# A gated mix of sliding-window attention and a token MLP: a new written order, a 128-column last piece, gate logits off TensorE

## The chip, the cores and the metric

The kernel runs on one core of a Trainium2 chip. The metric is the device time of one execution in microseconds; the median of three executions of the kernel before is 200.21 us (199.88 to 200.73). A core has five engines that run side by side [...]: TensorE (PE; its weight loads are listed apart as PEld), ScalarE (ACT), VectorE (DVE), GpSimd (POOL), and SyncE (SP), which here issues all DMA transfers. Matrix products land in PSUM, eight banks of 128 partitions by 512 fp32 values; all other on-chip data is in SBUF.

## The reference, cut to what matters

S = 2048 tokens, D = 512, 32 heads of 16, a window of 256 keys, F = 1376 hidden units. All inputs and the output are bf16.

```python
g = sigmoid((x * gate_w).sum(-1, keepdims=True))          # one gate per token
q, k, v = heads(x @ wqkv)                                 # 32 heads of 16
p = softmax(where(0 <= i - j < 256, q @ k.T / 4, -1e9))   # i query token, j key token
a = (p @ v) @ wo
h = layernorm(x)                                          # the same x as above
u = gelu(einsum("bsd,sf->bdf", h, w1) + b1)               # the MLP mixes tokens, not features
b = transpose(einsum("bdf,fs->bds", u, w2) + b2)          # back to tokens by features
return g * a + (1 - g) * b
```

## The kernel before, in words

Tokens are cut into 16 tiles of 128 and into 4 blocks of 512. The work is a list of named tasks. Each task belongs to one engine and issues one or a few instructions:

- `xta0.n.g` and `xtc0.n.g`: TensorE transposes of the first four token tiles (four 128x128 transposes each) and their copies to SBUF, line 606 and 599. The other three blocks are loaded already transposed by DMA (`xt1` to `xt3`).
- `q`, `k`, `v` chains (`project`, line 700; `chain`, line 653): products over four chunks of D. A chain is cut into steps; `q1_0.2` is the step of chain q1 of block 0 that begins with product 2. For block 0 the first weight chunk is applied to tokens 0 to 255 and 256 to 511 in two products of 256 columns, so these chains have five steps. `qc`, `kc`, `vc` are the copies out of PSUM; `qc` multiplies by a parity pattern so that two heads share a product.
- `sj.v0` to `sj.v3`, `sj.C`: scores of query tile j, and of the corners of its window (lines 923 and 1017); `e...` their exponentials on ACT, `m...` the window masks (line 901), on DVE or POOL; `pvj.i` the products with V (line 1073); `n1` to `n4` and `nz` the transposes and scalings on DVE that bring the result back into `xo`.
- `bs`, `ba`, `pow`, `h`: layernorm statistics and result. `u0` to `u10`: the first MLP product, 16 products a chain in steps of two. `ub`: its bias. `gelu`: one pass over all of it on ACT. `y0` to `y14`: second MLP product (11 products) and the attention's `wo` product (4) in one PSUM bank, `f` the final scale and bias, `o` the store. Tile 15 is cut into two pieces of 256 columns, `y15l` and `y15r` (line 1282).
- The gate's logits: for the first `NGP` = 1 blocks by 16 TensorE products with one column each (`gate0`, line 797), for the others by `gl`, one multiply with accumulation on DVE per token tile, which reads `gwr`, a copy of `gate_w` in every partition (load `gw`). `gatem` limits, `gatee` exponentiates, `ez` spreads them.

TensorE works in several tilings. A plain step uses the whole array. Score steps use four strips of 32 rows, `pv` steps four strips of 32 columns, corners both. A step of `q`, `k`, `v`, `u` or `y` is issued plain, or, where the name of the attention step before it stands in `THEN`, as four products of 32 output columns each, which then run side by side. In what follows "tiled steps" are these.

**What sets the order.** Each engine's order is written out by hand in `PLAN` (line 189), with the PSUM bank or buffer number that a task takes after the colon. `arrange` (line 85) only merges the five lists: it walks them with assumed costs (`SWITCH`, `LATENCY`, `BLOCK`) and decides the order in which instructions are emitted between engines, and where a POOL task gets a wait for a recent DVE task (line 1312 on). The order on each engine is that of `PLAN`. Every engine runs its list strictly in order, so a task that waits holds up all behind it.

**Start.** DVE clears `zeros`, 128x512 in the later `ug` buffer; TensorE multiplies zeros (`warm`, five products of 512 columns, `warmb`, three of 256; line 589) while the first loads are under way. SP issues `x0.0 x0.2 wqk0 wqk1 wqk2 wqk3 x1.4 xt1 wv x2.8 bias xt3 ...` in this order.

## Time and profile before

| | |
|---|---|
| median of the runs | 200.21 us |
| the profiled execution's own time | 199.82 us |
| its span (first to last instruction) | 198.1 us |
| PE busy | 193.0 us, 4058 products |
| ACT busy | 169.0 us |
| DVE busy | 156.5 us |
| POOL busy | 80.0 us |
| products with a full-clock record | from 6.92 us on |

How to read it: a product is issued before the one ahead of it has drained, so busy times of PE overlap and a busy PE is not PE at its peak. The distance from the start of one task's first product to the start of the next task's first product is what a task costs the PE queue. The groups list an instruction's busy time, its mean duration, and the idle time of its engine before it. 1.72 us of the profiled execution lie outside the span.

### The profile page before, as it was taken

The numbers are of one execution on the slowest core, as the hardware profiler recorded it, in microseconds if no ns is written. First come the engines' busy times: TensorE is split into PE (matmuls) and PEld (weight loads), VectorE is DVE, ScalarE is ACT, GpSimd is POOL, SyncE is SP. The second block draws the span as 40 slices with busy tenths as digits, with TensorE's granted clock in tenths as the row PEclk, the third lists the DMA queues.
The fourth block names the chain that finished last, engine by engine and source line by source line (L and its number), as shares of the span: only waits on it lengthen the run. The fifth ranks groups of instructions, "written<-read, shape, count | busy, mean of one in ns | idle before, by whom it ended". The sixth has DMA issues, their size and how long they took to land. (4 is left out here: it accounts for less than half of the span.)

```text
span 198.1 us, 9100 instructions
## 1 busy us (share of the span) xinstructions
PE 193.0 (97%) x4058; PEld 93.3 (47%) x4058; DVE 156.5 (79%) x318; ACT 169.0 (85%) x198; POOL 80.0 (40%) x118
## 2 busy tenths in 40 slices
PE   7999999999999999999999999999999999999993
PEld 3643444353635445446543554344445354554572
DVE  1799888879998988986589799636867868869683
ACT  2369999999988996998999899899899989898632
POOL 6394897525344440214223200045069335452310
PEclk9999999999999999999999999999999999999999
DMA  5999798970060000001399770000211220200002
GB/s 156 294 284 232 131 319 278 346 187 0 8 174 18 18 0 3 3 5 32 98 364 367 280 210 3 26 26 30 68 37 58 60 68 22 62 30 30 30 3 83
DMA packets 23189, 22.02 MB, mean 111 GB/s; under 512 B 7566, under 2 KB 21262, under 8 KB 23150
## 3 DMA queue, kind: packets, MB, share of 16 engines
q1 hardware_dynamic: 23150, 21.44, 36.9%
q8 instruction: 32, 0.52, 1.1%
q14 instruction: 7, 0.06, 0.1%
HBM read 15.61 MB, written 2.10 MB: 89 GB/s over the span
## 5 line engine op out<-in xcount | busy, mean ns | idle before, releaser
L894 ACT ACTIVATE et<-ps 128x1024 bf16<-128x1024 f32 (+1 forms) x94 | 89.3, 1015 | 6.1 <-PE ps L942 2.4
L536 POOL TENSOR_SCALAR_AFFINE_SELECT et<-et 128x512 bf16<-128x512 bf16 (+2 forms) x63 | 46.7, 751 | 56.0 <-ACT et L894 40.9
L894 ACT ACTIVATE XT<-ps 128x1024 bf16<-128x1024 f32 (+1 forms) x60 | 58.1, 1011 | 7.3 <-PE ps L942 4.3
L670 PEld LDWEIGHTS <-wb 128*32 128x32 bf16 (+4 forms) x645 | 32.0, 97 | 34.5 <-issue 6.5
L670 PE MATMUL pb<-ug,wb 128*32 128x512 bf16 (+4 forms) x385 | 45.5, 366 | 0.0
L670 PE MATMUL pb<-h,wb 128*128 128x512 bf16 (+2 forms) x260 | 44.5, 381 | 0.0
L536 POOL TENSOR_SCALAR_AFFINE_SELECT XT<-XT 128x512 bf16<-128x512 bf16 (+1 forms) x28 | 20.0, 720 | 46.3 <-ACT XT L894 27.4
L670 PE MATMUL pb<-XT,wqkv 128*128 128x512 bf16 (+2 forms) x190 | 32.4, 372 | 0.4 <-DMA wqkv<-in_A_wqkv_dram 0.3
L1178 DVE STREAM_TRANSPOSE et<-ps 128x1024 f32<-128x1024 f32 (+1 forms) x17 | 20.1, 1183 | 11.9 <-PE ps L1087 11.1
L1087 PEld LDWEIGHTS <-VA 128*32 128x32 bf16 (+1 forms) x1056 | 20.1, 97 | 6.6 <-issue 1.5
L942 PE MATMUL ps<-QZ,KT 32*128 32x256 bf16 (+1 forms) x496 | 23.1, 265 | 0.0
L754 DVE TENSOR_TENSOR QZ<-pb,par 128x1024 bf16<-128x1024 f32 x16 | 19.5, 1221 | 3.2 <-PE pb L670 3.2
L670 PEld LDWEIGHTS <-wqkv 128*128 128x128 bf16 (+1 forms) x190 | 12.7, 98 | 14.6 <-DMA wqkv<-in_A_wqkv_dram 0.5
L670 PE MATMUL pb<-wo,xo 128*32 128x512 bf16 (+2 forms) x152 | 18.1, 375 | 0.0
L1087 PE MATMUL ps<-et,VA 128*32 128x128 bf16 (+2 forms) x624 | 17.9, 218 | 0.0
L942 PEld LDWEIGHTS <-KT 32*128 32x128 bf16 x496 | 7.4, 92 | 20.6 <-ACT et L894 10.7
L670 PE MATMUL pb<-wqkv,XT 128*128 128x512 bf16 (+1 forms) x70 | 16.5, 381 | 0.0
L974 DVE TENSOR_TENSOR et<-et,mask 128x512 bf16<-128x512 bf16 x26 | 13.3, 510 | 2.5 <-ACT et L894 2.4
L441 DVE TENSOR_SCALAR ot<-pb,c,c 128x512 bf16<-128x512 f32 (+1 forms) x11 | 8.6, 785 | 7.4 <-PE pb L670 7.3
L1087 PE MATMUL ps<-XT,VA 128*32 128x128 bf16 (+2 forms) x432 | 13.9, 215 | 0.0
L1087 PEld LDWEIGHTS <-VZ 128*32 128x32 bf16 x832 | 13.2, 98 | 0.7
L770 DVE BATCH_NORM_STATS2 stats<-xo 128x6 f32<-128x512 bf16 x16 | 10.7, 682 | 3.1 <-DMA xo<-in_A_x_dram 3.1
(76 smaller groups left out, 199.4 us busy)
## 6 DMA issues: line engine op xcount, KB each, us to landing
wb<-in_B_w_dram SPq DMA_DIRECT2D x8, 512.0 KB, 8.2
wb<-in_B_w_dram SPq DMA_DIRECT2D x2, 2048.0 KB, 9.2
VZ<-VA SPq DMA_DIRECT2D x26, 70.0 KB, 3.0
xo<-in_A_x_dram SPq DMA_DIRECT2D x3, 512.0 KB, 5.5
out_dram<-ot SPq DMA_DIRECT2D x12, 128.0 KB, 2.4
wb<-in_B_w_dram SPq DMA_DIRECT2D x4, 352.0 KB, 5.8
wqkv<-in_A_wqkv_dram SPq DMA_DIRECT2D x4, 256.0 KB, 5.0
wb<-in_B_w_dram SPq DMA_DIRECT2D x1, 1024.0 KB, 5.3
```

Source lines behind the costliest of these rows:

```text
L441: return nc.vector.tensor_scalar(out=out_, in0=in_, scalar1=scale, scalar2=bias, op0=ALU.mult, op1=ALU.add)
L536: return nc.gpsimd.affine_select(out=out_, in_=in_, pattern=[[0, n] for n in pattern] + [[step, HB]], compare_op=op, fill=0.0, base=base_, ...
L670: made.append(nc.tensor.matmul(buf(b)[c:z_, c0:c0 + w_], lhsT=lhsT[:, c:z_], rhs=rhs, start=(j == 0), stop=(j == n - 1), skip_group_check= ...
L754: lambda k=k, b=b: nc.vector.tensor_tensor(out=QZ[:, k, :, (i % NQ) * SB:(i % NQ + 1) * SB], in0=buf(b)[:, None, :].to_broadcast([P, 2, SB ...
L770: f"bs{t_}", {"DVE": 0.67}, lambda b=b, t_=t_: nc.vector.bn_stats(buf(b)[:], xo[:, t_, :]),
L894: lambda e=e, b=b, shape=shape: nc.scalar.activation(out=shape(buf(e)), in_=shape(buf(b)), func=ACT.Exp, scale=SCALE),
L942: made.append(nc.tensor.matmul(to[:, :, done:done + m], lhsT=keys(j if x == "A" else j - 1, k)[rows], rhs=q[rows], start=True, stop=True, ...
L974: made.append(nc.vector.tensor_tensor(out=v, in0=v, in1=m.to_broadcast(list(v.shape)), op=ALU.mult))
L1087: return lambda: nc.tensor.matmul(to(), lhsT=v() if callable(v) else v, rhs=buf(e)[rows, col:col + n], start=first, stop=last, tile_positi ...
L1178: lambda: nc.vector.transpose(out=view(buf(tr).bitcast(FP32)), in_=view(buf(o))), [last], takes=[tr], uses=[o],
```

## The change

1. `y15r` is cut into `y15m` and `y15r`, 128 columns each, with their own final scaling and store.
2. `zeros` is 128x128; the warming products read it four (or two) times over with a stride of zero. They have the same count and width.
3. `NGP` is 0: `gate0` is gone, and `gl0` to `gl3` join DVE's list. `gw` is issued much earlier.
4. All lists of `PLAN`, and `THEN`, are written anew: the order on every engine, the banks, and which of the copies and masks run on which engine. POOL has 12 `m...v` masks fewer and one corner mask more; DVE 12 more and one fewer.
5. The assumed costs of `arrange` are refined (`TURN`, `cost_of`, the cost of `gelu`).

The halves of the first Q and K products are in both kernels, since `project` is the same. What differs is their place: before, nine halves stand ahead of the first later step (`q1_0.2`), now thirteen, with `xta0.1.1` moved in behind the first four of them.

```diff
-SWITCH = 0.095
-BLOCK, AHEAD, FETCH, BUSY = 256, 80, 3.6, 3.0
-LATENCY = {"PE": 0.22, "ACT": 0.15, "DVE": 0.12, "POOL": 0.15, "SP": 2.0}
+TURN = {
+    "d": dict(d=0, s=0.100, p=0.100, c=0.098, h=0.100),
...
+BLOCK, AHEAD, FETCH, BUSY = 256, 80, 3.1, 3.5
+LATENCY = {"PE": 0.21, "ACT": 0.15, "DVE": 0.11, "POOL": 0.12, "SP": 2.0}
+def cost_of(t, e):
...
-            if new != mode:
-                t.cost += SWITCH
+            t.cost += TURN[mode][new]
...
 PLAN = dict(
     PE="""
-        warm:3 xta0.0.0:7 xta0.0.1:6 warmb xta0.1.1:4 xta0.1.0:5 q1_0.0:2 k3_0.0:3 k1_0.0:6 q3_0.0:1 k0_0.0:7
-        q3_0.1 q0_0.0:0 k3_0.1 q1_0.1 q1_0.2 k1_0.1 k3_0.2 k0_0.1 q0_0.1 q2_0.0:5 q1_0.3 q0_0.2 q1_0.4 q0_0.3
+        warm:5 xta0.0.0:6 xta0.0.1:4 warmb xta0.1.0:3 q3_0.0:2 q2_0.0:5 k1_0.0:6 q1_0.0:1 xta0.1.1:4
+        k0_0.0:7 k3_0.0:0 q3_0.1 k3_0.1 k0_0.1 q2_0.1 k1_0.1 q0_0.0:3 q1_0.1 q3_0.2 k3_0.2 q0_0.1 q3_0.3
...
-        y14.11 y14.13 y13.13 y15r.6 y15r.8 y15l.11 y15l.13 y15r.10 y15r.11 y15r.13
+        y14.11 y15l.4 y15m.2 y15l.6 y15m.4 y15m.6 y14.13 y15l.8 y15l.10 y15l.11 y15l.13 y15m.8 y15m.10
+        y15m.11 y15m.13 y15r.0:3 y15r.2 y15r.4 y15r.6 y15r.8 y15r.10 y15r.11 y15r.13
...
     DVE="""
-        const zeros bs3:1 xtc0.0.0 bs2:0 ba3 parity bs1:1 ba2 ba1 bs0:0 ba0 qc1_0 bs4:1 qc0_0 ba4 qc3_0 qc2_0 qc3_1
+        const zeros parity bs0:0 bs3:1 ba3 xtc0.0.1 xtc0.0.0 xtc0.1.0 bs1:1 ba0 ba1 bs2:0 qc3_0 bs5:1 qc0_0
+        qc1_0 gl0 gl1 ba2 qc2_0 ba5 bs6:0 ba6 gl3 h2 vc5 gl2 gatem0 h3 bs4:0 qc3_1 ba4 bs7:1 bs8:0 biasc ba8
...
     SP="""
-        x0.0 x0.2 wqk0 wqk1 wqk2 wqk3 x1.4 xt1 wv x2.8 bias xt3 x3.12 xt2 vs0 w1_02 w1_03 vs1 w1_22 vs2 gw w1_12
+        x0.0 x0.2 wqk0 wqk3 wqk1 wqk2 x1.4 wv gw xt1 xt3 bias x2.8 vs0 xt2 w1_20 w1_12 vs1 x3.12 w1_03 vs2
...
-    NGP = 1
+    NGP = 0
...
-    zeros = ug[:, 0, :]
+    zeros = ug[:, 0, 0:P]
...
-            nc.tensor.matmul(buf(wu)[:, 0:w], lhsT=zeros[:, 0:P], rhs=zeros[:, 0:w], start=True, stop=True)
+            nc.tensor.matmul(
+                buf(wu)[:, 0:w].rearrange("p (a b) -> p a b", b=P), lhsT=zeros,
+                rhs=zeros[:, None, :].to_broadcast([P, w // P, P]), start=True, stop=True,
+            )
...
-        parts = [("", 0, D)] if t_ < NT - 1 else [("l", 0, D // 2), ("r", D // 2, D)]
+        parts = [("", 0, D)] if t_ < NT - 1 else [("l", 0, D // 2), ("m", D // 2, 3 * D // 4), ("r", 3 * D // 4, D)]
```

## The prediction

> **What bounds the kernel.** I read the page's busy shares first, then the waits of TensorE, then the timeline of TensorE and of the tail.

> The busy shares:
> ```profile
> PE 193.0 (97%) x4058; PEld 93.3 (47%) x4058; DVE 156.5 (79%) x318; ACT 169.0 (85%) x198; POOL 80.0 (40%) x118
> ```
> PE is listed as busy all the time, which alone says little, since products overlap. TensorE's own waits say more:
> ```profile
> PE pb L591 <- DVE ug L518: 1.4, 1, 1.4
> PE pb L670 <- DMA wqkv<-in_A_wqkv_dram: 0.3, 1, 0.3
> PE pb L670 <- ACT XT L894: 0.2, 1, 0.2
> ```
> Three waits in 198 us: for the zeros, for the first weights, and once for ACT. So from the first real product at 6.57 the kernel is a TensorE queue with hardly a hole, and its time is: start of that queue, sum of the steps, tail. The prices of the steps are distances between starts in the timeline of PE (start, length, instruction):
> ```profile
> 23.02 0.54 PE L802 MATMUL pb<-gwc,XT 128*128 128x1 bf16 x16
> 23.43 1.02 PE L670 MATMUL pb<-wqkv,XT 128*128 128x512 bf16 x4
> ...
> 30.68 0.59 PE L670 MATMUL pb<-XT,wqkv 128*128 128x512 bf16 x2
> 31.21 0.41 PE L1087 MATMUL ps<-et,VA 128*32 128x128 bf16 x16
> ...
> 56.84 1.47 PE L670 MATMUL pb<-h,wb 128*128 128x512 bf16 x6
> 58.24 0.40 PE L942 MATMUL ps<-QZ,KT 32*128 32x256 bf16 x8
> 58.57 1.68 PE L670 MATMUL pb<-h,wb 128*128 128x512 bf16 x7
> ```
> The gate's 16 products cost 0.41. A plain step of two products, followed by another, costs 0.432 (median of the steps); followed by strips of columns 0.53 (30.68 to 31.21), so that change of tiling costs 0.10. Six products and a change take 1.40 (3 x 0.432 + 0.10), a score step 0.33. The tail:
> ```profile
> 194.40 0.60 PE L670 MATMUL pb<-wo,xo 128*128 128x256 bf16 x4
> ...
> 195.04 0.55 DVE L441 TENSOR_SCALAR ot<-pb,c,c 128x256 bf16<-128x256 f32 x1 [0.61 <-PE pb L670]
> ...
> 195.61 0.33 SPq L1305 DMA_DIRECT2D out_dram<-ot  x1
> ```
> Last product out at 195.00, final scaling to 195.59, store, end at 198.1.

> I laid the medians of such distances, per kind of step and kind of the next one, under the whole list of before: 186.62 from 6.57 to the end of the last product's slot. The trace takes 188.26. The 1.64 between are waits too small to be listed: 0.16 while the clock comes up (two halves at 0.19 for 0.109), 0.25 at `s10.v0`, 0.13 at `y9.6`, 0.11 at `pv1.3`, 0.08 at `k0_3.2`, 0.07 at `y1.2`, the rest crumbs.

> [...] 256 zero columns take 0.213 at 4.6, 256 real ones 0.109 after 7.0, and the full-clock record starts at 6.92. [...] the trace has no plain 128-column product at full clock. [...] the gate's products, each with a 128x128 weight load, pass at 25 ns, so the load is no floor. [...] The last store has rows of 512 B before, 256 B after; no run here shows the latter.

> **The change, part by part, on the queue of PE.**

> Gate: `gate0` leaves, -0.40. `gl0` to `gl3` come to DVE at 0.7 to 0.8 each (the accumulating multiply is 8.3 us for 12, and its read-out 81 ns), 3.1 in all; 12 masks `m...v` move from POOL to DVE at 0.45 to 0.51 (5.7), one corner mask goes back. DVE gets some 8 us more on 156.5 of 198, POOL loses as much. This costs nothing while DVE keeps ahead of the bank it must free; without that cover it would cost up to the 3.1 at the start, where DVE has 9.58 of 10 us busy between 10 and 20. I followed that stretch: `qc1_0` ends about 13.5, `gl0` and `gl1` 14.8, `qc2_0` 16.0, `gl3` and `h2` 17.8, `vc5` 18.4; PE wants the bank of `vc5` (`v14.0`) at 19.2. Covered by 0.8.

> Changes of tiling: 167 before, 163 after. Every score, corner and `pv` group still has its own; what goes is four direct changes between plain and tiled steps (13 to 9), -0.40. Tiled steps are 67, not 74; leaving a tiled step costs 0.107 rather than 0.095, and that happens 22 times, not 27: -0.06.

> Last tile: 15 products of 256 columns become 30 of 128. By the slope between 512 and 256 columns, 0.416 ns a column, one is 0.056: 30 x 0.056 - 15 x 0.109 = +0.05. [...] I take 0.05, for the 25 ns above.

> Start: the weights `wqk0` land at 6.53 in both, so the first product stays at 6.57. But before, all 16 transposes are over by then; after, `xta0.1.1` stands behind four products: 4 x 0.056 = +0.22 at full clock (0.43 at half). The weights now come as 0, 3, 1, 2, landing at 6.53, 7.19, 7.84, 8.44 by the trace. The first step with chunk 1, `q3_0.2`, comes up at 8.21, the first with chunk 2 at 8.76: 0.3 to spare. The shorter clearing of zeros (0.27 for 512 columns, so some 0.15 less) lets warming start earlier, hidden behind `x0.0`, which lands at 3.74.

> SP queue: `wv` and `gw` now go ahead of `xt1`. By the pace of 512 KB in 1.7 us (8.44 to 10.12) `wv` lands near 12, wanted at 12.75 (`v0.0`); `xt1` about 2.3 later than the 12.05 of before, so 14.3, wanted at 15.9 (`v5.0`). `vs13` waits for `vc13` (about 35.7) and holds `w1_13`, `w1_01`, `w1_00` behind it until 37 to 39; at 1.7 each the last lands about 43, wanted at 46 (`u3.0`). All hidden, the thinnest by 0.7.

> Sum of the steps after, rounding included: 186.00, thus -0.62. Tail: the scaling of 128 columns is 0.13 shorter (0.81 at 512, 0.55 at 256)[...]. The middle piece is scaled on ACT and issued before the last is scaled, so SP is free.

> Small waits: 1.48 of before beyond the clock's 0.16. The new order has its own. Two are in sight: after gelu, ACT frees bank 6 for `s9.v3` some 0.15 to 0.2 late, and `s9.v2` after it 0.1 late (gelu with its two table loads takes 7.8; the exponentials follow at 0.905 each); and `y15l.11` comes 2.67 after `pv15.2`, whose way through DVE takes 2.8. That makes 0.4; I give the rest another 1.1, so as many as before. The profiled execution goes from 199.82 to 199.07. The median of the runs lies 0.39 above it: 199.46, said as **199.4**.

> **Rivals.** Half a per cent, 1.0 us here, is about what a measurement can tell from no change: faster means under 199.2, slower over 201.2.

> *The waits shrink.* If the new order has 0.4 of small waits instead of 1.5, the time is 198.4. For it: between 13 and 31 I find ACT and DVE ready 0.1 to 0.5 ahead of every bank that PE wants. Against: 0.1 is little, and some will fail.

> *The waits grow.* PE comes earlier to gelu and to each score step while ACT's 169 us stay; DVE has 8 more. One microsecond more of waits gives 200.4, no change; it needs 0.1 at ten of the 60 score steps.

> [...]

> [...] Before 6.92, PE idles 0.46 between the last transpose and the first product; after, with `xta0.1.1` gone from there, 0.89. [...] It decides once the full-clock record starts past about 10 rather than near 7. Against it: the warming itself is unchanged[...].

> That the change does not do what it says is true in part: the halves are in both kernels; only their order changed, priced above.

> **How the numbers follow.** Forecast 199.4 (198.9 to 199.9): 0.40, a little over half below 199.2. Waits shrink: 0.20. Waits grow: 0.24, of it 0.04 beyond 201.2. [...] Clock late: 0.10. Faster 0.22 + 0.20 = 0.42; slower 0.10 + 0.04 = 0.14; the rest, 0.44, is no change. The range 198.3 to 201.0 leaves out the late clock, the tail of the growing waits and some 0.04 below.

> **What would show it.** Right: L802 gone from PE; first real product at 6.5 to 6.6; the full-clock record near 7; the last product out about 0.6 earlier than 195.00; the last scaling near 0.42; the 128-column products 0.056 apart. Wrong: waits of PE on ACT or DVE that add up to over 2.5 us, a wait on `wqkv`, `XT` or `wb` loads, a full-clock record near 10, or a last store that takes over 0.3 longer from issue to the end.

## The result

The kernel after takes 205.46 us, median of four executions (204.32 to 205.84), against 200.47 of four of the kernel before (199.88 to 201.06). The ratio is 1.0258, with a 95% interval of 1.0228 to 1.0289. It is slower by 5 us; the forecast was 199.4, with a range up to 201.0. Single executions of a kernel can run over 1.5% above its fastest one; the ratios here and below leave these out, the medians include them.

The profiled execution took 205.32 us with a span of 203.6. From the page of after, the busy times and the chain of work that ended last by engine:
```profile
PE 193.9 (95%) x4018; PEld 92.5 (45%) x4018; DVE 158.3 (78%) x338; ACT 168.3 (83%) x198; POOL 72.6 (36%) x108
...
PE 79%; DMA 12%; SPq 4%; ACT 2%; issue 2%; DVE 0%; ACTq 0%
```
TensorE is no longer busy without a break: 95% of a longer span, and the chain leaves it for transfers (DMA 12%) and for "issue", time in which an engine waited for nothing that the profile shows. The waits of TensorE of after (instruction and line, what ended the wait, us in total, times, longest):
```profile
PE ps L1115 <- issue: 2.1, 3, 1.2
PE pb L698 <- DMA wqkv<-in_A_wqkv_dram: 1.2, 2, 0.9
PE pb L616 <- DVE ug L543: 1.2, 1, 1.2
PE pb L698 <- DMA wb<-in_B_w_dram: 1.0, 2, 0.5
PE ps L1115 <- DMA VZ<-VA: 0.9, 1, 0.9
PE pb L636 <- DMA xo<-in_A_x_dram: 0.3, 1, 0.3
PE ps L970 <- issue: 0.2, 1, 0.2
```
The waits of before held three lines, two of them of the start and one of 0.2. Here five lines are new (both on "issue", and those on `wb`, `VZ` and `xo`), and the one on `wqkv` has grown from 0.3 to 1.2. Apart from the wait for the zeros at the start, no wait on ACT or DVE, which the prediction's rivals spoke of, is among them.

I laid the prediction's step prices under the trace of after, as was done for before. The sum of the differences is the span's difference:

| | before | after | difference |
|---|---|---|---|
| first real product | 6.57 | 6.08 | -0.49 |
| steps, by their prices | 186.62 | 186.00 | -0.62 |
| waits between them | 1.64 | 8.53 | +6.89 |
| end of the last slot to the end of the span | 3.26 | 2.98 | -0.28 |
| span | 198.1 | 203.6 | +5.5 |

The steps are taken at the prediction's prices here, so that line checks nothing by itself; the single prices are compared further down. The tail moved the way that was worked out. What the prediction took as equal grew by 6.9 us. The waits by place, the step named being the first that comes late:

| step | us | what is late |
|---|---|---|
| `q3_0.3` | 1.03 | load of `wqk2`, landed at 9.26 |
| `u3.0`, `u7.0` | 0.68, 0.65 | loads `w1_00`, `w1_10`, landed at 47.3 and 51.5 |
| `pv7.1` to `u9.14` | 1.23 | copy `vz7`, landed at 114.2 and 114.4 |
| `u6.2`, `pv8.2`, `y14.4`, `pv15.2` | 0.43, 1.34, 0.74, 0.69 | nothing that the profile shows |
| all others | 1.74 | as many as before |

So 3.6 us are transfers, 3.2 have no releaser. Both kinds can be seen in the timeline of TensorE of after (start, length, operation, tiles, count, idle time before it and what ended it):
```profile
113.10 0.23 PE L1115 MATMUL ps<-XT,VA 128*32 128x128 bf16 x4
114.20 0.41 PE L1115 MATMUL ps<-et,VZ 128*32 128x64 bf16 x8 [0.87 <-DMA VZ<-VA]
...
118.09 0.20 PE L1115 MATMUL ps<-et,VZ 128*32 128x64 bf16 x2
119.44 0.23 PE L1115 MATMUL ps<-et,VZ 128*32 128x64 bf16 x6 [1.16 <-issue]
```
The second wait falls in the middle of eight products of one kind on the same tiles: two went, six followed 1.35 us later. None of the six has a semaphore to wait for in the trace.

**The transfers.** SP's queue in the timeline of after, around `vs13`:
```profile
25.72 0.59 SPq L511 DMA_DIRECT2D wb<-in_B_w_dram  x1
36.62 0.46 SPq L746 DMA_DIRECT2D VS<-VA  x1
37.13 1.76 SPq L747 DMA_DIRECT2D VS<-VA  x1
38.93 1.70 SPq L511 DMA_DIRECT2D wb<-in_B_w_dram  x3
...
42.01 1.50 SPq L511 DMA_DIRECT2D wb<-in_B_w_dram  x2
```
SP stands from 26.3 to 36.6 for `vc13`, and five loads of `w1` stand behind it. That is as predicted. The prediction followed the first three of them and let the last of these, `w1_00`, land at 43; it landed at 47.3. The fourth, `w1_10`, landed at 51.5. And around `vz7`:
```profile
104.16 0.37 SPq L1301 DMA_DIRECT2D wb<-in_B_w_dram  x1
104.59 0.51 SPq L756 DMA_DIRECT2D VZ<-VA  x1
105.14 0.59 SPq L757 DMA_DIRECT2D VZ<-VA  x1
```
`w2_1`, 2 MB, is issued just ahead of the two copies of `vz7`, so they share the queue with it and take 9.6 and 9.2 us. The pages give the median of all such copies from issue to landing, first before, then after:
```profile
VZ<-VA SPq DMA_DIRECT2D x26, 70.0 KB, 3.0
```
```profile
VZ<-VA SPq DMA_DIRECT2D x26, 70.0 KB, 7.1
```
In before `vz7` was issued behind the other 2 MB load, `w2_0`, and its first copy took 9.1 us too; but that was at 96.46, and it landed at 105.54, well ahead of its use. What the new order changed is how late it stands.

**The waits without a releaser.** Instructions are data too: the page of after lists two DMA queues of the kind "instruction". The larger of them, in after and then in before (packets, MB, share):
```profile
q8 instruction: 31, 0.51, 1.1%
```
```profile
q8 instruction: 32, 0.52, 1.1%
```
Each packet is of 16384 bytes. In after 31 come with 8036 weight loads and products, from the first packet to the last one per 258 of them on the mean; in before, with 32, one per 254. So I take this queue for TensorE's, and a packet for 256 rows of TensorE's list, which is the `BLOCK` of the kernel's own planner. Such packets need not cost anything: in before no wait of TensorE is put down to "issue". The records of the queue in the trace of after say when they do. For each wait without a releaser: TensorE's place in its list of instructions, the last packet before it, and when TensorE went on:

```
row of the list   row mod 256   packet          goes on    after its end
2477              173           76.87-77.80     79.19      1.39
4266              170           117.08-118.06   119.44     1.38
7585              161           189.29-190.83   192.16     1.33
7841              161           193.21-194.31   195.89     1.57
```
All four stand at nearly the same place of a block, and TensorE goes on 1.3 to 1.6 us after the packet's end. For three of the four the packet starts 1.0 to 1.2 us after TensorE has entered the block before it; for the one at `pv8.2`, with the loads of `w2_2` under way, it started 2.4 us after. A packet takes 0.9 to 1.5 us. Added up, 1.05 + 0.95 + 1.4, my estimate is that a block has to last 3.4 us, or TensorE waits for the rest, and longer where the packet starts or moves more slowly. The blocks ahead of these four waits lasted 2.9, 3.45 (`pv8.2`), 3.3 and 3.1 us; the shortest of before, 3.43, ended without one. A plain step of 0.43 us uses 4 of the 256, a tiled one 16, but a group of 128 `pv` products in 1.36 us uses them all. The mean over the kernel is 6 us a block; whether two dense groups fall into one block and the next is a matter of where the boundaries lie. The estimate is my reading of one trace; the experiments below put it to the test.

### The profile page after: what moved, and what is told of

Same layout as the page of the kernel before. It is cut to its first block, busy times and chain, and to the rows that moved or that the text cites. A ratio compares the mean times of both kernels' runs of the same rounds, so it can differ in the third digit from the quotient of the medians.

```text
span 203.6 us, 9014 instructions
## 1 busy us (share of the span) xinstructions
PE 193.9 (95%) x4018; PEld 92.5 (45%) x4018; DVE 158.3 (78%) x338; ACT 168.3 (83%) x198; POOL 72.6 (36%) x108
## 4 chain that ended last, share of the span: by engine, by line
PE 79%; DMA 12%; SPq 4%; ACT 2%; issue 2%; DVE 0%; ACTq 0%
PE pb L698 57%; PE ps L1115 10%; PE ps L970 8%; DMA VZ<-VA 5%; DMA wb<-in_B_w_dram 5%; DMA wqkv<-in_A_wqkv_dram 3%; PE ps L1070 2%; SPq L747 1%; SPq L511 1%; ACT et L922 1%; SPq L495 1%; ACT XT L922 1%; SPq L479 0%; ACT VA L630 0%; PE ps L1026 0%
## 5 line engine op out<-in xcount | busy, mean ns | idle before, releaser
L922 ACT ACTIVATE et<-ps 128x1024 bf16<-128x1024 f32 (+1 forms) x104 | 98.4, 1012 | 8.0 <-PE ps L970 3.7
L561 POOL TENSOR_SCALAR_AFFINE_SELECT et<-et 128x512 bf16<-128x512 bf16 (+2 forms) x57 | 42.4, 755 | 73.0 <-ACT et L922 47.5
L922 ACT ACTIVATE XT<-ps 128x1024 bf16<-128x1024 f32 (+1 forms) x50 | 49.5, 1032 | 5.3 <-PE ps L970 5.3
L698 PE MATMUL pb<-h,wb 128*32 128x512 bf16 (+2 forms) x326 | 45.0, 381 | 1.0 <-DMA wb<-in_B_w_dram 1.0
L698 PE MATMUL pb<-ug,wb 128*32 128x512 bf16 (+6 forms) x309 | 45.2, 362 | 0.0
L561 POOL TENSOR_SCALAR_AFFINE_SELECT XT<-XT 128x512 bf16<-128x512 bf16 (+3 forms) x24 | 17.3, 731 | 41.2 <-DVE et L935 12.5
L698 PE MATMUL pb<-wo,xo 128*32 128x512 bf16 (+3 forms) x168 | 17.9, 370 | 0.0
L698 PE MATMUL pb<-wqkv,XT 128*128 128x512 bf16 x64 | 16.7, 381 | 0.0
L935 DVE TENSOR_TENSOR et<-et,mask 128x1024 bf16<-128x1024 bf16 (+1 forms) x19 | 12.0, 646 | 4.9 <-ACT et L922 4.9
L1115 PE MATMUL ps<-et,VZ 128*32 128x64 bf16 x608 | 13.0, 193 | 2.0 <-issue 1.2
```

The lines of the kernel that those rows point to most:

```text
L561: return nc.gpsimd.affine_select(out=out_, in_=in_, pattern=[[0, n] for n in pattern] + [[step, HB]], compare_op=op, fill=0.0, base=base_, ...
L698: made.append(nc.tensor.matmul(buf(b)[c:z_, c0:c0 + w_], lhsT=lhsT[:, c:z_], rhs=rhs, start=(j == 0), stop=(j == n - 1), skip_group_check= ...
L922: lambda e=e, b=b, shape=shape: nc.scalar.activation(out=shape(buf(e)), in_=shape(buf(b)), func=ACT.Exp, scale=SCALE),
L935: return nc.vector.tensor_tensor(out=v, in0=v, in1=m[:, None, :].to_broadcast([P, n, w]), op=ALU.mult)
L1115: return lambda: nc.tensor.matmul(to(), lhsT=v() if callable(v) else v, rhs=buf(e)[rows, col:col + n], start=first, stop=last, tile_positi ...
```

## The experiments

Ratios are against runs of the kernel before on the same chip.

### The transfers, one at a time

```diff
 vz7_first:
-        vz8:1 w2_1 vz7:0 vz11:2 w2_2
+        vz8:1 vz7:0 w2_1 vz11:2 w2_2
```

> The kernel after, with one change in SP's list: the two copies of vz7 are issued ahead of the 2 MB load w2_1 instead of behind it. Theory of the queue: pv7.1 waited 0.9 us for VZ because its copies sat behind w2_1 (issued 104.6, landed 114.4, where such copies took 3 us in the kernel before). The wait on VZ goes, u9.14 starts about 1.2 us earlier, and with it gelu and the y steps: about 1.2 us faster than the kernel after (205.5 to 204.3). Rival, a hidden wait: gelu, the last w2 load or ACT sets the start of y4.0 anyway, the wait moves to y4.0 or s9.v1 and under 0.4 us is won.

203.93 us, 1.0135 (1.0045 to 1.0224), with executions from 201.68 to 205.50. The wait on `VZ` is gone. `pv8.2`, on the same stretch, waits 0.48 in place of 1.34.

```diff
 vs13_late:
-        w1_02 vs13 w1_13 w1_01 w1_00 vz2:1 w1_10 w1_11 vz6:2
+        w1_02 w1_13 w1_01 w1_00 vz2:1 w1_10 w1_11 vs13 vz6:2
```

> The kernel after, with one change in SP's list: the copies vs13, which wait for vc13 until 36.6 us, are issued behind w1_11 instead of ahead of w1_13, w1_01, w1_00, w1_10, w1_11. Theory of the queue: SP stood from 26.3 to 36.6 and these five loads came 10 us late; u3.0 waited 0.68 us and u7.0 0.65 us for them. Both waits go: about 1.3 us faster than the kernel after (to 204.2). Rival: PE at 46 to 51 us is also held by ACT (score banks), so that the waits on wb go but 0.5 us or more comes back as waits on ACT at s3 and s4.

204.99 us, 1.0208 (1.0145 to 1.0270). The waits at `u3.0` and `u7.0`, 1.33 us, are gone from the profile, yet the median fell by 0.5 only, which four executions from 202.73 (the profiled one) to 205.43 can't tell from nothing. `pv8.2` now waits 1.53, and `pv7.1` 1.1. In the profiles each order of SP does what it was made for, and `vs13_late` gives a part of what it earns back behind it.

### Two attempts at the waits without a releaser

```diff
 untile: THEN without these
-    s5.v0 s8.v2 pv7.0 pv7.1 pv14.1 pv14.3
 uncluster: the four steps of pv8 moved from between pv7.2 and q3_3.0
-        pv7.2 pv8.0:6 pv8.1 pv7.3 pv8.2 pv8.3 q3_3.0:5
+        pv7.2 pv7.3 q3_3.0:5
-        q1_3.2 k0_3.2 y4.0:3
+        q1_3.2 k0_3.2 pv8.0:6 pv8.1 pv8.2 pv8.3 y4.0:3
```

> The kernel after, with six names taken out of THEN (s5.v0, s8.v2, pv7.0, pv7.1, pv14.1, pv14.3): the q, u and y steps after them are issued plain, two instructions pairs instead of eight. Nothing is left out of the computation. Theory of instruction supply: PE takes its instructions in blocks of 256 from DRAM (31 packets of 16 KB on the instruction queue), a block arrives some 2.4 us after it is asked for, and dense stretches of pv and tiled steps use a block up in 1.4 us; the stretches at u6.2 (0.43 us), pv8.2 (1.34), y14.4 (0.74) and pv15.2 (0.69) waited for that. With fewer instructions in front, u6.2, y14.4 and pv15.2 lose most of their waits and pv8.2 part of it: 1.2 to 2.0 us less waiting, some 0.8 us given back by about eight more changes of tiling; net 0.4 to 1.2 us faster than the kernel after. Rival, a semaphore that the profile does not show (banks, masks on POOL or DVE): the waits stay within 0.2 us of where they are, and the kernel is 0.8 us slower than after.

> The kernel after, with the four steps of pv8 moved from between pv7.2 and pv7.3 to behind k0_3.2, seven q and k steps later; all else is as it was. Theory of instruction supply: pv7.2 to pv8.3 are 320 pairs of instructions within some 1.8 us of work, more than a block; with 3 us of q and k steps between them the 1.34 us wait inside pv8.2 goes and the kernel is 1.0 to 1.4 us faster than after. Rival (pv8 waits for its own inputs, VZ copies vz8 or masks m8): those were long there by the trace, but if it is so, the wait inside pv8 stays where pv8 goes or shrinks by the 3 us that it is later, with PE idle for another releaser; a second rival, n18 on DVE three us later holds bank 6 for s9.v1 and gives back 0.5 us or more.

`untile`: 211.74 us, 1.0561 (1.0514 to 1.0607). `uncluster`: 209.44 us, 1.0459 (1.0427 to 1.0491). Both missed by far. In `untile` the waits at `u6.2`, `y14.4` and `pv15.2` went; the one at `pv8.2` moved on into `pv8.3` and doubled, and others came at places that nothing had been done to. From its timeline of TensorE, one that is new and the one in `pv8.3`:
```profile
98.59 0.29 PE L1115 MATMUL ps<-et,VA 128*32 128x128 bf16 x6 [1.39 <-issue]
...
124.44 0.35 PE L1115 MATMUL ps<-et,VA 128*32 128x128 bf16 x12 [2.67 <-issue]
```
In `uncluster`, `pv8` still waits 0.6 inside, and a new wait of 1.4 without a releaser comes at 189.7. But a part of its loss is not of that kind. From its waits,
```profile
PE pb L698 <- DVE et L1206: 1.5, 1, 1.5
```
is the wait of `y4.0` on DVE, which had itself stood 4.83 us for the result of `pv8`. That is close to the second rival that was named, though it hits another step. And behind this wait TensorE's granted clock was 0.5 from 123.91 to 127.32: products of 512 columns came 0.43 apart in place of 0.216, some 1.7 us more in all. What both have in common is that they change how many instructions precede a given piece of work: plain steps in place of tiled ones take instructions out (174 in `untile`), in `uncluster` the seven steps that now follow `pv7.3` are issued tiled, 84 instructions more, and every later boundary moves. So the next runs move the boundaries and nothing else.

### Moving the boundaries alone, in the kernel before

The order of before has no such wait. Its warming products can be cut finer without changing the columns that they multiply.

```diff
 before_rows16 and before_rows88 (for warm, then for warmb):
-        lambda: warming(5, 512)
+        lambda: warming(10, 256)      # rows88: (40, 64)
-        lambda: warming(3, 256)
+        lambda: warming(6, 128)       # rows88: (12, 64)
```

> The kernel before with the warming products cut finer at the same total of columns (10 of 256 and 6 of 128 columns in place of 5 of 512 and 3 of 256): 8 more products, 16 more instructions on TensorE ahead of all real work, nothing else changed. Theory SUPPLY (TensorE is handed its instructions in blocks of 256, and a block that is used up in less than about 3.5 us leaves TensorE idle until the next one is there): every block boundary after the start moves 16 instructions towards the beginning of the work. Laid over the step times of before, that gives waits without a releaser near 63.6 (0.65 us), 152.9 (0.45) and 172 (0.4) and some smaller ones, together 2.0 (1.0 to 3.0, with 3.3 to 3.7 us for a block): 202.4. Theory SLACK (the waits of the new order come from engines, banks and loads that are late): where boundaries fall doesn't matter, 200.4 as before, no new waits.

> As the kernel with 16 more instructions, but 40 and 12 products of 64 columns: 44 more products, 88 more instructions at the start, the same total of columns. SUPPLY: waits without a releaser near 95 (1.5 us), 115 (1.0), 153 (1.9), 173 (1.6), 184 (0.9) and 196 (0.9), together 8.4 (6.8 to 10): 208.8. SLACK: 200.4.

`before_rows16`: 201.20 us, 1.0054 (1.0039 to 1.0069). `before_rows88`: 207.44 us, 1.0349 (1.0296 to 1.0401). Finer warming at the start costs up to 7 us at the other end of the kernel. Step by step against the trace of before, the differences of `before_rows88` over 0.5 us are +1.09 at 95.4, +2.13 at 114.9, +1.05 at 154.3, +0.96 at 174.1, +0.90 at 184.3 and +0.67 at 197.1: the six places that were named. Of `before_rows16` they are +0.28 at 63.8, +0.21 at 153.4, +0.69 at 172.2 and +0.40 at 181.5; all three named places, each smaller or larger than said. The waits of TensorE of `before_rows88`:
```profile
PE pb L670 <- issue: 3.6, 3, 2.0
...
PE ps L1087 <- issue: 1.3, 2, 0.8
PE ps L942 <- ACT et L894: 1.0, 1, 1.0
```
and the first of them in its timeline, in the middle of a run of equal products (x1, then x23),
```profile
95.43 0.39 PE L670 MATMUL pb<-h,wb 128*32 128x512 bf16 x1
96.72 1.48 PE L670 MATMUL pb<-h,wb 128*32 128x512 bf16 x23 [0.90 <-issue]
```
where the timeline of before has the same 24 in one piece:
```profile
95.38 1.48 PE L670 MATMUL pb<-h,wb 128*32 128x512 bf16 x24
```
(The last line of the waits, put down to ACT, is at the boundary near 154 and ends 1.47 us after a packet; I count it with the others.)

Then the prediction's own first step, done alone. It leaves out three quarters of the products of `gate0`, so the logits of the first 512 tokens are summed over a quarter of the features.

```diff
 gate_quarter:
-                    for t_ in range(4) for ck in range(4)
+                    for t_ in range(4) for ck in range(1)
 gate_quarter_rows: the same, and warming(8, 320), warming(12, 64)
```

> The kernel before, with gate0 of 4 products in place of 16: the logits of the first 512 tokens are summed over the first quarter of the features only, the rest is left out. It takes 0.3 us (12 products of 25 ns) off TensorE, with DVE, POOL and SP untouched. The prediction's own step, the gate's products taken off TensorE's queue at their price: 200.4 - 0.3 = 200.1. SUPPLY: 24 instructions fewer from 23 us on move the later boundaries the other way; waits near 89 (1.0 us) and 184 (1.6), together 2.6 (2.2 to 3.3), less 0.3: 202.7.

> As gate_quarter (same part left out), with the 24 instructions put back ahead of all real work: warming in 8 products of 320 and 12 of 64 columns. SUPPLY: all boundaries after 23 us where they are in the kernel before, so no such waits, and the 0.3 us is earned: 200.1. Prediction's step alone: 200.1 too. If it is as slow as gate_quarter, SUPPLY falls.

`gate_quarter`: 202.14 us, 1.0086 (1.0047 to 1.0125). `gate_quarter_rows`: 200.12 us, 1.0005 (0.9982 to 1.0029). In both traces the step is 0.30 shorter, as priced. The first is 0.9% slower all the same, 1.7 us, and with 24 instructions put back far ahead of it that is gone. From the timeline of `gate_quarter`:
```profile
94.08 0.38 PE L670 MATMUL pb<-h,wb 128*32 128x512 bf16 x1
95.50 0.61 PE L670 MATMUL pb<-h,wb 128*32 128x512 bf16 x7 [1.04 <-issue]
```
One of the two waits that were named is one block later than said, and the one near 184 is not in this execution. Whether `gate_quarter_rows` earned its 0.3 its interval can't tell; in the profiled execution, the slowest of twelve, products ran at half pace until 10.3, which is told of below.

### The kernel after without its waits on transfers, then with other boundaries

```diff
 after_loads:
-        x0.0 x0.2 wqk0 wqk3 wqk1 wqk2
+        x0.0 x0.2 wqk0 wqk1 wqk2 wqk3
-        q0_1 q3_0.3 q3_0.4 k1_0.2 q1_0.2 k0_0.2 k1_0.3
+        q0_1 k1_0.2 q1_0.2 k0_0.2 q3_0.3 q3_0.4 k1_0.3
 and the edits of vz7_first and vs13_late
 after_loads_flags: after_loads, and in THEN
+    s10.v2 s13.v2 s14.v0 s6.C
-    pv12.3 s13.v0 s3.v2 s6.v2
```

> The kernel after with its four waits on transfers taken away by order alone: vz7 ahead of w2_1; vs13 behind w1_11; the weights in the order wqk0 wqk1 wqk2 wqk3; q3_0.3 and q3_0.4 behind k1_0.2 q1_0.2 k0_0.2. Theory LOADS PLUS SUPPLY: against before, steps -0.62, tail -0.33 (the scaling 0.19 shorter and the last store 0.14, by five profiles of each kind), no waits on loads, and supply waits near 64 (0.7 us), 77 (0.4), 114 (0.5), 187 (0.3) and 190 (0.2), together 2.1 to 3.7: 201.3 to 202.9, likeliest 202.2. Theory LOADS ALONE (the waits without a releaser follow from the loads and go with them): 200.1 - 0.95 = 199.2.

> As after_loads, with eight names changed in THEN, found by laying blocks of 256 instructions over the step times so that no block is used up too soon: s10.v2 s13.v2 s14.v0 s6.C in, pv12.3 s13.v0 s3.v2 s6.v2 out. The order of the tasks is the same, the number of tiled steps nearly so. SUPPLY: steps -0.40 against before, tail -0.33, supply waits 0.6 to 1.4 (near 114 and 188): 199.9 to 200.9, likeliest 200.3, thus about 2 us faster than after_loads. Rival (which steps are tiled matters only by the 0.2 us of their own prices): no faster than after_loads, 202.2 to 202.4.

`after_loads`: 201.65 us, 1.0078 (1.0049 to 1.0107), within what was said, and 3.8 below the kernel after: about the share of the transfers, worked out as 3.6. (The two profiled executions lie 2.45 apart: the one of `after_loads`, the slowest of seven, began 0.9 later.) `after_loads_flags`: 202.00 us, 1.0096 (1.0066 to 1.0126), 1.7 above what was said. Its profile does show what the edit was made for. The waits without a releaser are 2.63 us in `after_loads` (0.70 at `u6.2`, 0.77 at `pv8.2`, 0.74 at `y14.4`, 0.42 at `pv15.2`) and 1.19 in `after_loads_flags`; from the waits of the latter,
```profile
PE ps L1026 <- issue: 0.7, 1, 0.7
```
is the only one listed. From the first product to the last its profiled execution is 1.4 us shorter than that of `after_loads`. But it began 0.3 later (first product at 7.31, against 6.99, and 6.57 in before), and other small waits make 2.4 us in it, not 1.6 as in before. The remaining wait, 0.92 at `y13.2`, hung on a packet that took 1.57 us where I had reckoned with 0.95. The profiles are of one execution each, the slowest of seven and the second fastest of six, and executions of these kernels lie up to 2 us apart, so the gain in the profile is not shown as a gain in time.

### Work that costs nothing

If these waits are supply, then more work inside the block that is used up too soon is free, since the next block is under way meanwhile.

```diff
 fill_wait (fill_else: "y4" and "y1"), in chain, on top of after_loads:
-                for j in range(a, z):
+                for j in ([0] * 3 if a == 0 and name in ("y14", "k2_3") else []) + list(range(a, z)):
```

> after_loads with useless work in two blocks of instructions that are used up too soon: the first product of y14 and of k2_3 is issued four times in place of once (each time from zero, so the sum is the same), 6 more products of 512 columns at 0.216 us, 1.30 us in all, and 12 more instructions. SUPPLY: the block lasts 0.65 us longer while the next one is under way, so the waits at pv8.2 (0.77 us in the profile of after_loads) and y14.4 (0.74) shrink to 0 to 0.2 each, by 0.8 to 1.2 together: 0.1 to 0.5 slower than after_loads, 201.8 to 202.1 if that repeats its 201.65. Rival (these waits come from something just ahead of them, whatever went before): the waits stay, 1.3 slower, 202.95.

> The counterpart: the same 6 useless products at y4 and y1, in blocks that are used up slowly. SUPPLY: nothing swallows them, the waits at pv8.2 and y14.4 stay, 1.3 slower than after_loads: 202.95, and 0.8 to 1.2 slower than fill_wait. Rival: the same time as fill_wait.

Step by step against the trace of `after_loads`: in `fill_wait`, `k2_3.0` is 0.65 longer and the wait at `pv7.3` to `pv8.2` 0.77 shorter; `y14.0` is 0.65 longer and the one at `pv14.3` to `y14.4` 0.74 shorter. Both waits are gone, and this trace shows no cost of the 1.30 us of added work. From the waits of `after_loads`,
```profile
PE ps L1115 <- issue: 1.3, 3, 0.6
```
is gone in `fill_wait`, whose only line on "issue" is
```profile
PE ps L970 <- issue: 0.2, 1, 0.2
```
In `fill_else`, `y4.0` and `y1.0` are 0.65 longer each and nothing behind them is shorter up to the next boundary with a wait. At `pv8.2`, ahead of its additions, it still waits 0.50 (its packet took 2.0 us, 2.6 in `after_loads`), where `fill_wait` does not. Behind them the picture is mixed: the wait at `y14.4` is 0.68 smaller, without any work in that block, and the one at `pv15.2` 0.51 larger. So the 12 added instructions alone move a wait from one boundary to the next, and `y14.4` taken alone shows nothing. Over both boundaries, from just ahead of `y14.0` to the last product, `fill_else` takes 0.08 less than `after_loads`, and `fill_wait` 0.26 less with 0.65 of work more in it.

In times (six executions each, five and three of them in the ratios), `fill_wait` has 202.93 (1.0120, 1.0080 to 1.0161) and `fill_else` 204.96 (1.0147, 1.0102 to 1.0191). That is the order that was said, but the intervals overlap, and both are above the figures given. The profiled executions are the fastest of `fill_wait` (200.99) and one of the slowest of `fill_else` (205.81). What tells the two apart is these traces, one of each.

### The last piece alone

```diff
 before_piece, in the kernel before:
-        parts = [("", 0, D)] if t_ < NT - 1 else [("l", 0, D // 2), ("r", D // 2, D)]
+        parts = ... [("l", 0, D // 2), ("m", D // 2, 3 * D // 4), ("r", 3 * D // 4, D)]
 with y15m in the places of y15r, and the new y15r beside it to the end
 before_piece_zeros: and the warming on 128x128 zeros
 piece_early: before_piece_zeros, y15m finished before y15r begins
 piece_early_flags: piece_early, in THEN s13.v2 for s13.C
```

> The kernel before with the last 256 columns of the last tile cut into two pieces of 128, each with its scaling and store, nothing else of the change. By the prediction's figure of 0.056 us for a product of 128 columns: products +0.04, scaling -0.19, last store -0.14 by the profiles so far: 199.8 against 200.1. [...]

> As before_piece, and the warming on 128x128 zeros as in the kernel after. Warming begins 0.2 us earlier (1.17 against 1.38), behind x0.0's load, which lands at 3.5 to 3.7: nothing by itself. If it moves the full clock ahead of the first product where this now comes at half clock, 0.1 to 0.2 more: 199.6 to 199.8.

> before_piece_zeros with y15m finished ahead of y15r, as in the kernel after, in place of both at the end: so the middle piece's store is issued 0.4 us earlier and SP is free when the last scaling ends. In before_piece_zeros SP issued the last store 0.33 us after the scaling (0.02 in before), and from the scaling's end to the end of the span it took 2.71 (2.38 in the kernels of the new order). If the collision on SP was what ate up the gain: tail 0.3 shorter than before_piece_zeros, 0.33 shorter than before, 199.8 against 200.2. If not: 200.0 to 200.2.

> As piece_early, with s13.v2 in THEN in place of s13.C: the steps of the same price, but 24 instructions of tiled steps are issued later, so that the boundary of row 7337 no longer falls on s14.C, where before_piece waits 0.52 and before_piece_zeros 0.35. SUPPLY: that wait goes and none takes its place, or 0.1 at pv13.2: 199.5 to 199.6. If the wait is not supply: as piece_early.

The ratios are 0.9998 (0.9984 to 1.0013), 0.9990 (0.9972 to 1.0007), 1.0002 (0.9985 to 1.0019) and 1.0005 (0.9990 to 1.0021), medians of 200.26, 199.99, 200.14 and 200.73 us. None can be told from before, so no version that beats both kernels was found; each beats the kernel after by some 5 us.

The parts are as priced. In the five profiles each of the first kernels of both orders, the last product's start to the end of the last scaling is 0.67 us with the piece of 128 columns and 0.86 with 256, and from there to the end of the span 2.38 and 2.52. In the old order the second gain was lost at first: the last store was issued 0.18 and 0.33 us after its scaling in the first two kernels, behind the middle piece's store on SP, and 0.07 after it in `piece_early`, with 2.57, 2.72 and 2.46 to the end. The first gain met a supply wait: TensorE waits at `s14.C`, where before does not, in three of the four, and the flags took that wait away as said:

```
                     place of the wait   row    us from the row before
before_piece         s14.C (180.84)      7326   0.49
before_piece_zeros   s14.C (180.54)      7326   0.32
piece_early          s14.C (180.74)      7297   0.45
piece_early_flags    u4 (97.25)          3478   0.33
```
(The place in `u4` is in `before_piece_zeros` too, with 0.33. In the last two traces some 30 of TensorE's records are missing ahead of these rows.) But in `piece_early_flags` SP took 1.71 us over two stores that took 0.81 before, and so issued the last one 0.95 after its scaling. What 0.3 us is worth can't be shown against such scatter.

## Why the prediction was wrong, by its own steps

**What it worked out held.** The gate's products are gone from the trace, and the twelve that were taken away alone shorten the step by 0.30, by the 25 ns that were used. Products of 128 columns come 0.056 apart: in after, eleven of them from 199.77 to 200.39, which is what the slope between the wider ones gave. The lines of its tail, with the last piece's scaling and store:
```profile
199.77 0.78 PE L698 MATMUL pb<-ug,wb 128*128 128x128 bf16 x11
...
200.39 0.39 PE L698 MATMUL pb<-wo,xo 128*128 128x128 bf16 x4
200.82 0.41 DVE L466 TENSOR_SCALAR junk<-pb,c,c 128x128 bf16<-128x128 f32 x1 [0.64 <-PE pb L698]
201.26 0.33 SPq L1333 DMA_DIRECT2D out_dram<-junk  x1
```
The prediction took the last store, of rows of 256 B, to last as long as the one of 512 B rows before; from the end of the last scaling to the end of the span it is 0.14 sooner (2.38 and 2.52 us). `xta0.1.1` behind four products costs 0.22, as said. DVE's cover of 0.8 for the gate's logits was enough: no wait of TensorE on DVE follows the start.

**Mis-sized: the first weights.** "8.44" for the fourth load, hence "0.3 to spare" for `q3_0.3`, was carried over from the trace of before. In after the fourth load landed at 9.26, 15 of its 16 parts by 8.12. TensorE, which began 0.49 earlier than the prediction had it, came up to `q3_0.3` that much earlier and so waited 1.03. In the executions that were profiled the first load landed anywhere between 5.7 and 7.3. A margin of 0.3 is inside that scatter.

**Mis-sized: the loads of `w1`.** The step named the stall at `vs13`, its place and its length, and failed on what comes after. "At 1.7 each the last lands about 43" counts from the moment that SP is free. In after SP issued `w1_13` at 38.93; it landed at 43.26, 4.3 us later, then `w1_01` at 45.44 and `w1_00` at 47.34. So the time from issue to landing of the first was left out, and the pace was 2.0. And the loads were followed to `u3.0` only; `w1_10`, behind them and two more copies, made `u7.0` wait. That `vz7` stands behind 2 MB of `w2_1` was in the list and not looked at. Together with the weights these are 3.6 us, and `after_loads`, where their waits are gone, took 201.65 in place of 205.46.

**Missing: the supply of instructions.** "Small waits" were taken as a sum that a new order leaves about the same, "as many as before". For the crumbs that was right: 1.74 against 1.64. The term that it put at nothing is the supply of TensorE's own instructions, 3.2 us in the trace of after. The profile of before shows no wait of that kind, because before never ran short. It was not out of sight. The diff changes `BLOCK, AHEAD, FETCH, BUSY`; the planner that merges the lists counts TensorE's instructions in blocks of 256 and lets each come `FETCH` (3.6 us before, 3.1 after) later than the block ahead of it is entered, and later still while loads are under way. I listed these constants and followed everything else through the new order. The price was there in part: blocks of before that last 3.4 us without a wait, and 32 packets on the page for 8116 weight loads and products. Over all eighteen traces of this case the pattern holds: each of the 33 waits of TensorE of 0.2 us or more that the profile puts on "issue" ends 1.1 to 1.6 us after a packet, at place 157 to 173 of its block (one at 130, in a trace that lacks some 30 records).

Removing the gate is the plainest case. Its 16 products were priced at -0.40, which is their time. Taking out twelve of them alone cost 1.7 us, since all boundaries behind them moved; with the boundaries put back, the cost was gone.

**The rivals.** "The waits grow" had the sign, at 0.04 for over 201.2, with ACT and DVE as its cause, which is not what happened. The late clock, which the prediction gave 0.10 because TensorE would idle 0.89 rather than 0.46 ahead of its first product, did not happen in the profiled execution of after: its full-clock record starts at 5.43 (6.92 in before). It did in two of the nine profiled executions with the new start, `untile` and `fill_else`, where products ran at half pace until 10.2 and 10.7, and in none of the seven with the old start and warming products of 128 columns or more. With 64-column warming it came in part in `before_rows88` and in full in `gate_quarter_rows`. So that rival was real, and adds to the scatter of the new order; how often it comes in executions that were not profiled stays open.

**What stays open.** The budget of `after_loads` against before is -0.62 for the steps, -0.27 for the tail, +2.63 for supply, +0.9 for other small waits and +0.42 for a later start: +3.1, the difference of the spans of the two profiled executions. The median is only 1.45 above before. Which of these terms is smaller in the other executions can't be seen. That the new order would beat the old one if it were never short of instructions is therefore not shown.

## What to carry to other kernels

Where TensorE is the bound and its list is long, count its instructions as well as its time: mark every 256th weight load or product on the timeline, and ask whether each block lasts as long as the next one needs to arrive (3.4 us here, by an estimate from four waits of one trace); an edit that adds or removes a few instructions moves all boundaries behind it, and can cost or earn more than its own work. A wait on "issue" in the middle of a run of equal products, at the same place of a block each time (157 to 173 in these traces, with one exception), is how it shows, and it can be tried by adding a few useless instructions at the very start. A copy that stands behind a large load on the same queue can take three times as long (3.0 and 9.6 us here), so follow each queue to its end, not to the first use.
